# A delta-rule attention and SwiGLU kernel: the loads of v(2), v(3) and K(5) are issued behind the first two pieces of the output weights

## The chip, the cores and the metric

The kernel runs on one core of a Trainium2 chip. The metric is the device time of one execution in microseconds (us), the median of several runs. A profile is one execution taken by the hardware profiler. Its times count from the start of its span.

## What is computed

The reference is a delta-rule recurrence, whose output is reshaped into tokens and sent through a SwiGLU feed-forward block:

```python
# q, k, v: (4, 8, 768, 48) float32; beta: (4, 8, 768) float32
k_n = k / (np.linalg.norm(k, axis=-1, keepdims=True) + 1e-06)
for t in range(S):
    kt, vt, bt = (k_n[:, :, t], v[:, :, t], beta[:, :, t, None])
    y[:, :, t] = np.einsum('bhd,bhde->bhe', q[:, :, t], state)
    v_old = np.einsum('bhde,bhd->bhe', state, kt)
    state = state + bt[:, :, :, None] * np.einsum('bhd,bhe->bhde', kt, vt - v_old)
x = np.ascontiguousarray(y.transpose(0, 2, 1, 3)).reshape(B * S, H * D)
g = x @ w_gate                      # (3072, 384) @ (384, 1536)
silu = g * (1.0 / (1.0 + np.exp(-g)))
out = silu * (x @ w_val) @ w_out    # (1536, 384)
```

The three weight matrices reach the kernel as 64-bit floats, so they are converted to float32 on the chip.

## The kernel before

**Chunks.** The 768 steps are cut into 12 chunks of 64 steps, c = 0 to 11. For each chunk, q, k and v of all 32 heads are loaded, and the recurrence over the chunk is solved with small matrix products. `advance(c)` (line 948 on) is that solution in four steps; its last steps make the 256 tokens of the chunk, which the feed-forward block takes up. "K(5)" below is the load of the k rows of chunk 5, "v(2)" that of the v rows of chunk 2.

**Weights in pieces.** The weights are staged as 42 pieces (`pieces`, lines 200 to 207), numbered in the order of conversion. Pieces 0 to 23 are 128 rows by 256 columns of the gate weights (even numbers) and the value weights (odd numbers). Pieces 24 to 29 are the last 512 columns of both. Pieces 30 to 41 are the twelve 128-row tiles of the output weights. `stage(n)` (line 246) issues the DMA of a piece on SyncE's queue, at line 260, into a place that is shared by several pieces (`place_of`). `freed_by` lists for each piece the pieces that may be staged once it is converted: 24 after 13, 25 after 15, 26 after 17, 28 after 18, 27 after 19, 30 after 21, 31 after 23, 32 after 28, 33 after 29, and from there on each piece after the fourth before it. `freed_by` only places the call; on the chip the DMA itself waits until the last instruction that touches its place is done.

**Conversion.** `convert(ns)` (line 280) converts the pieces of a group. ScalarE does the two activations of `power_step` (lines 272 and 278: the high word scaled into the weight tile, the low word into a "power" tile). VectorE does a shift (line 289), a bit operation (line 297) and the addition of the power (line 309). Between lines 297 and 309, `convert` calls `power_step` for the pieces that follow, so ScalarE takes up a following piece before VectorE's additions for this one. The power tiles are shared: the power of piece 24 lies where those of 22 and 23 lie.

**The first feed-forward chunks.** Chunks 0 and 1 go through `gate_val(c, f, ...)` (line 1402): for two 128-column blocks f and f+1, six matmuls of the gate weights (line 1410), ScalarE's silu (line 1419), six matmuls of the value weights (line 1410), VectorE's product (line 1421). The pairs (c, f) run in the order (0,0), (0,2), (0,4), (0,6), (1,0), (1,2), (1,4), (1,6), (0,8), (1,8), (0,10), (1,10). Their products go round four PSUM banks, two for each pair: the gate product of a pair needs the bank that the silu two pairs earlier has read, the value product the bank that the product at line 1421 two pairs earlier has read. `fill` and `chain` put conversions between the pairs. Then `output` (matmuls at line 1437) multiplies by the output weights for chunks 0 and 1. From chunk 2 on, `gate_val_fast` and `output_fast` do the same with fewer products (matmuls in the helpers at lines 1314 and 1520).

**The inversion.** Each pair of chunks needs a small triangular system inverted (`invert`, line 849). For chunks 2 and 3 it begins between the pairs (0,6) and (1,0): two copies on ScalarE (line 856), two transposes on VectorE (line 569), a power on GpSimd (line 860).

**Order.** Each engine executes its instructions in the order in which the program emits them; the schedule is written by hand. SyncE's queue carries nearly all loads. Each `load_v` is four DMAs (line 186), each `load_k` two (line 140). In `advance(1)`, which is emitted between the conversions of pieces 6 to 17, `load_v(2)` and `load_v(3)` are called at the end of the third step and `load_k(5)` in `of_state` of the fourth.

Of the kernel before, what the change touches and what calls it, by code (L numbers as in the profile page):

```python
# [20 lines left out]
def kernel(  # L21
# [34 lines left out]
    FT = DFF // 128  # L56
# [17 lines left out]
    def ps_pair(name, tag):  # L74

        return pairs_of_banks[tag]
# [19 lines left out]
    AHEAD = 4  # L96
# [12 lines left out]
    def kn_of(c):  # L109
        return knp[c if c < AHEAD else c % 2]  # L110
# [4 lines left out]
    def rows_freed_by(c):  # L115
        return c - AHEAD if c < K_BLOCKS else c - 2
# [18 lines left out]
    def halves(x, c, b):  # L135
        return x[NB * b : NB * b + NB, :, c * C : (c + 1) * C, :]

    def load_heads(t, x, c, dmas=(nc.sync,)):
        for b in range(2):
            dmas[b % len(dmas)].dma_start(  # L140
                out=t[64 * b : 64 * b + 64, :, :, 0:D].rearrange(
                    "p bp h d -> p (bp h) d"
                ),
                in_=halves(x, c, b).rearrange("bp h p d -> p (bp h) d"),
            )

    def load_k(c, dmas=(nc.sync,)):
        load_heads(kn_of(c), k, c, dmas)
# [31 lines left out]
    def load_v(c):  # L180
        vin[c] = work.tile([128, 2, NB, NJ, D], FP32, name="vin", bufs=2)
        for b in range(2):
            src = halves(v, c, b).rearrange("bp (j par) p d -> par p (bp j) d", par=2)
            for par in range(2):
                s = 64 * (b ^ par)
                nc.sync.dma_start(
                    out=vin[c][s : s + 64, par].rearrange("p bp j d -> p (bp j) d"),
                    in_=src[par],
                )
# [10 lines left out]
    pieces = []  # L200
# [6 lines left out]
        pieces.append((wo_sb, moe_w_out, t, 0, DM))  # L207
    assert DFF == 1536 and KT == 3 and DM <= PIECE and 2 * HH * C == 4 * PIECE

    staged, powers, places = {}, {}, {}  # L210

    def words(tile_):
        return tile_.bitcast(U32)

    zt_flat = [words(t).rearrange("p c h i -> p (c h i)") for t in ztp]
    places = {
        "z0": zt_flat[0],
        "z1": zt_flat[1],
        "wo": words(wo_sb).rearrange("p t d -> p (t d)"),
    }  # L220
# [25 lines left out]
    def stage(n, after=None, queue=nc.sync):  # L246
        _, src, t, f0, m = pieces[n]
        name, lo = place_of[n]
        if name not in places:
            if name == "p_sb":  # L250
                places[name] = words(p_places[0])
            else:
                places[name] = work.tile(
                    [128, 2 * PIECE], U32, name="staged", tag=name, bufs=1
                )
        place = places[name][:, lo : lo + 2 * m]
        staged[n] = place
        if after is not None:
            nc.gpsimd.tensor_copy(place[:, 0:1], staged[after][:, 0:1])
        queue.dma_start(  # L260
            out=place, in_=src[t * 128 : (t + 1) * 128, f0 : f0 + m].bitcast(U32)
        )

    def power_step(n):
        if n in powers or n not in staged:
            return
        dst, _, t, f0, m = pieces[n]
        power = words(hp[10 + (n // 2 % 4 if n < N_HALF else (0, 2, 3, 1)[(n + 2) % 4])])
        power = power[:, n % 2 * m : n % 2 * m + m] if n < N_HALF else power[:, 0:m]
        powers[n] = power  # L270
        words_of = staged[n].rearrange("p (f two) -> p f two", two=2)
        nc.scalar.activation(
            dst[:, t, f0 : f0 + m],
            words_of[:, :, 1].bitcast(FP32),
            ACTF.Copy,
            scale=2.0**-112,
        )
        nc.scalar.activation(power, words_of[:, :, 0], ACTF.Copy, scale=2.0**-29)

    def convert(ns, ahead=6):  # L280

        work_of = []
        for n in ns:
            dst, _, t, f0, m = pieces[n]
            power_step(n)
            place = staged.pop(n)[:, 0:m]
            work_of.append((dst[:, t, f0 : f0 + m].bitcast(U32), place, powers.pop(n)))
        for dst, place, _ in work_of:
            nc.vector.tensor_scalar(
                out=place,  # L290
                in0=dst,
                scalar1=3,
                scalar2=None,
                op0=ALU.logical_shift_left,
            )
        for dst, place, _ in work_of:
            nc.vector.scalar_tensor_tensor(
                out=dst,
                in0=dst,
                scalar=0x80000000,  # L300
                in1=place,
                op0=ALU.bitwise_and,
                op1=ALU.bitwise_or,
            )
        for n in range(ns[-1] + 1, ns[-1] + 1 + ahead):
            if n < min(N_HALF, len(pieces)) or ns[-1] + 3 > n < len(pieces):
                power_step(n)
        for dst, _, power in work_of:
            nc.vector.tensor_tensor(out=dst, in0=dst, in1=power, op=ALU.add)  # L309
        for n in ns:  # L310
            for later in freed_by.get(n, ()):
                stage(later)


# [38 lines left out]
    def half_of(x):  # L353
        return slice(64 * x, 64 * x + 64)

    def head_of(x):
        return slice(64 * x, 64 * x + D)

    def every():
        for bp in range(NB):  # L360
            for j in range(NJ):
                for n, (par, b) in enumerate(ORDER):
                    yield bp, j, par, b, bp == 0 and j == 0
# [429 lines left out]
    def recur(p, m=D):  # L793
        p = p[:, :, 0 : NB * NJ * m]
        return p.rearrange("p x (bp j d) -> p x bp j d", bp=NB, j=NJ)
# [152 lines left out]
    def advance(c):  # L948
# [171 lines left out]
                        yield MORE  # L1120
        if c + 2 < NCH:
            if c == 1:
                load_v(2)
                load_v(3)
            elif c > 1:
                late_loads.append(lambda: load_v(c + 2))
        yield
# [15 lines left out]
        def of_state():  # L1143
            p_s = recur(ps_pair("p_s", "px"))
            for bp, j, par, b, first in every():
                nc.tensor.matmul(  # L1146
                    p_s[head_of(par) if c > 0 else half_of(par), b, bp, j],
                    kn[half_of(b), bp, 2 * j + par, 0 : D if c > 0 else DP],
                    uu[half_of(b), par, bp, j],
                    start=first,  # L1150
                    stop=True,
                    skip_group_check=True,
                )
            if c > 0:
                nc.vector.tensor_tensor(out=state, in0=state, in1=p_s, op=ALU.add)
                spent.append(1.4)
            else:
                nc.scalar.copy(state, p_s)
            for later in range(AHEAD, NCH):
                if rows_freed_by(later) == c:  # L1160
                    if c < 2:
                        load_k(later)
                    else:
                        late_loads.append(lambda: load_k(c + 2))

        if 0 < c < NCH - 1:
            of_state()
# [49 lines left out]
        if c == 0:  # L1217
            of_state()
            yield
# [398 lines left out]
    def converts(n):  # L1618
        if todo:
            convert(todo[:n])  # L1620
            del todo[:n]

    def converts_first(*ns):

        convert(list(ns), 0)
        for n in ns:
            todo.remove(n)
# [92 lines left out]
    def point(c):  # L1720

        mine = c < NCH and steps("advance", c) < 4 and may_advance(c)
        if mine and steps("advance", c) > 0:
            step("advance", advance, c)
        elif not prep_step(c - 1) and mine:
            step("advance", advance, c)

    def finish(c):

        if c < NCH:  # L1730
            while not may_advance(c):
                fill_some(1000)
                prep_step(c - 1)
            while steps("advance", c) < 4:
                step("advance", advance, c)
# [196 lines left out]
```

## Time and profile before

| | |
|---|---|
| median of 3 runs | 692.09 us (691.2 to 692.13) |
| the profiled execution | 692.09 us, of which the span of the profile is 690.4 us |
| VectorE busy | 414.0 us (60% of the span) |
| ScalarE busy | 262.6 us (38%) |
| GpSimd busy | 194.3 us (28%) |
| mean rate of the DMAs | 90 GB/s |

The profiled execution took as long as the median, and 1.69 us of it lie outside the span. A row of a timeline has the start and the duration in us, the engine (PE is TensorE, PEld its weight loads, DVE is VectorE, ACT ScalarE, POOL GpSimd, SPq SyncE's queue), the line, the operation, the tile written and the tiles read, shapes, and the number of instructions merged. In brackets stands the idle time of the engine just before, and what ended it. A tile is named by its memory: `zt`, `wo_sb`, `p_sb` and `staged` are the places into which weight pieces are loaded, `h_f` and `last_h` those of powers and hidden values, `vin` v, `kn` k.

### The profile page before, as it was taken

To read this page: it belongs to the slowest core of one execution; us is meant where nothing else is said; L and a number is where in the kernel's file an instruction comes from. 1 tells how busy PE (TensorE), PEld (TensorE's weight loads), DVE (VectorE), ACT (ScalarE), POOL (GpSimd) and SP (SyncE) were. 2 spreads that over 40 slices of the span, in tenths; PEclk is the share of its full clock that TensorE was granted. 3 is DMA by queue.
4 is the path that set the end of the run, shared out by engine and by line. 5 is a ranking of instruction groups with operands and counts; after the bars stand their busy time and mean duration, and the time that the engine had idled before them with its cause. 6 is when DMAs were issued, how large, how long until landed. Compare 5 with 4: busy or idle time off the path is not lost.

```text
span 690.4 us, 24601 instructions
## 1 busy us (share of the span) xinstructions
PE 675.4 (98%) x10836; PEld 629.7 (91%) x10836; DVE 414.0 (60%) x874; ACT 262.6 (38%) x557; POOL 194.3 (28%) x310
## 2 busy tenths in 40 slices
PE   8899999999999999999999999999999999999997
PEld 4788788756999999999999999999999999999997
DVE  7888578898657664647456546655555544433341
ACT  4777576214432523344323245232144242142230
POOL 5111031105883128820037830308810000000000
PEclk9999999999999999999999999999999999999999
DMA  9658925017561621464432373253253121221210
GB/s 133 160 162 204 245 75 161 1 34 174 129 113 19 116 79 40 100 110 93 88 77 71 69 137 73 56 103 77 55 110 69 56 64 47 56 63 47 71 45 24
DMA packets 143851, 62.24 MB, mean 90 GB/s; under 512 B 122977, under 2 KB 126049, under 8 KB 143745
## 3 DMA queue, kind: packets, MB, share of 16 engines
q1 hardware_dynamic: 141536, 60.19, 38.5%
q8 instruction: 85, 1.39, 0.9%
q10 hardware_dynamic: 2080, 0.39, 0.4%
q0 software_dynamic: 128, 0.10, 0.1%
q14 instruction: 22, 0.17, 0.1%
HBM read 53.58 MB, written 7.08 MB: 88 GB/s over the span
## 4 chain that ended last, share of the span: by engine, by line
PE 82%; DMA 8%; ACT 3%; SPq 3%; DVE 2%; issue 1%; POOL 0%; POOLq 0%; DVEq 0%; ACTq 0%
PE ffn L1314 42%; PE ffn L1520 20%; PE ffn L1437 4%; DMA h_f<-in_moe_w_val_dram 2%; PE ffn L1410 2%; PE p_px L977 2%; PE p_py L960 2%; DMA wo_sb<-in_moe_w_val_dram 2%; SPq L140 1%; PE p_py L1134 1%; PE p_px L1043 1%; PE p_px L1146 1%; PE p_px L527 1%; PE p_py L1207 1%; DMA wo_sb<-in_moe_w_gate_dram 1%
## 5 line engine op out<-in xcount | busy, mean ns | idle before, releaser
L1314 PE MATMUL ffn<-x_ffn,wg_sb 128*128 128x128 f32 x840 | 128.4, 275 | 0.5 <-ACT ffn L1370 0.3
L1314 PE MATMUL ffn<-x_ffn,wv_sb 128*128 128x128 f32 x840 | 128.1, 275 | 0.0
L1314 PEld LDWEIGHTS ffn<-x_ffn,wg_sb 128*128 128x128 f32 x840 | 111.1, 192 | 1.0 <-ACT ffn L1370 0.7
L1314 PEld LDWEIGHTS ffn<-x_ffn,wv_sb 128*128 128x128 f32 x840 | 110.7, 192 | 0.0
L1349 DVE TENSOR_TENSOR h_f<-sil,ffn 128x256 f32<-128x256 f32 x120 | 49.6, 418 | 83.6 <-ACT sil L1344 82.2
L1344 ACT ACTIVATE sil<-ffn 128x256 f32<-128x256 f32 x120 | 45.8, 383 | 128.1 <-PE ffn L1314 127.3
L1520 PE MATMUL ffn<-wo_sb,h_f 128*128 128x192 f32 x480 | 83.4, 327 | 0.0
L860 POOL TENSOR_TENSOR n_b<-mb,half 128x32 f32<-128x32 f32 x5 | 30.0, 6005 | 178.2 <-DVE mb L569 178.2
L1520 PEld LDWEIGHTS ffn<-wo_sb,h_f 128*128 128x128 f32 x480 | 78.1, 190 | 0.3
L605 POOL TENSOR_TENSOR zb<-zb,tmp 128x31 f32<-128x31 f32 (+15 forms) x124 | 72.6, 586 | 9.7
L599 POOL TENSOR_TENSOR tmp<-zb,mb 128x31 f32<-128x31 f32 (+15 forms) x124 | 67.0, 540 | 16.9 <-DVE mb L586 7.4
L1481 DVE TENSOR_TENSOR ffn<-ffn,p_sb 128x512 f32<-128x512 f32 x58 | 40.4, 696 | 48.7 <-ACT ffn L1370 47.3
L1314 PE MATMUL ffn<-x_t,h_f 128*128 128x128 f32 x480 | 61.0, 280 | 0.2 <-ACT ffn L1327 0.2
L1314 PEld LDWEIGHTS ffn<-x_t,h_f 128*128 128x128 f32 x480 | 56.3, 191 | 2.1 <-ACT ffn L1327 0.4
L1481 DVE TENSOR_TENSOR o_sb<-o_sb,ffn 128x192 f32<-128x192 f32 x49 | 17.2, 352 | 64.0 <-PE ffn L1520 61.4
L1327 ACT COPY ffn<-ffn 128x512 f32<-128x512 f32 x30 | 17.1, 571 | 60.8 <-PE ffn L1314 60.8
L1410 PE MATMUL ffn<-x_ffn,wg_sb 128*128 128x256 f32 x144 | 34.5, 385 | 2.9 <-DVE wg_sb L309 1.4
L1478 DVE TENSOR_TENSOR h_f<-h_f,h_f 128x256 f32<-128x256 f32 x60 | 29.6, 496 | 11.8 <-PE ffn L1520 10.6
L1520 PE MATMUL ffn<-last_k,h_f 128*128 128x192 f32 x200 | 36.0, 327 | 0.0
L1410 PE MATMUL ffn<-x_ffn,wv_sb 128*128 128x256 f32 x144 | 33.9, 383 | 0.4 <-DVE h_f L1421 0.4
L1410 PEld LDWEIGHTS ffn<-x_ffn,wg_sb 128*128 128x128 f32 x144 | 26.5, 190 | 7.6 <-DVE wg_sb L309 2.2
L1520 PEld LDWEIGHTS ffn<-last_k,h_f 128*128 128x128 f32 x200 | 32.9, 190 | 0.1
(323 smaller groups left out, 1123.3 us busy)
## 6 DMA issues: line engine op xcount, KB each, us to landing
h_f<-w_s SPq DMA_DIRECT2D x60, 256.0 KB, 2.8
p_sb<-w_s SPq DMA_DIRECT2D x27, 256.0 KB, 2.8
vin<-in_v_dram SPq DMA_DIRECT2D x48, 96.0 KB, 3.3
out_dram<-o_sb SPq DMA_DIRECT2D x48, 96.0 KB, 2.2
kn<-in_k_dram SPq DMA_DIRECT2D x20, 192.0 KB, 4.8
zt<-in_moe_w_out_dram SPq DMA_DIRECT2D x6, 384.0 KB, 3.8
qpad<-in_q_dram SPq DMA_DIRECT2D x36, 64.0 KB, 3.1
w_s<-h_f SPq DMA_DIRECT2D x7, 256.0 KB, 4.2
```

The lines of the kernel that those rows point to most:

```text
L599: engine.tensor_tensor(out=t_v, in0=zb[:, 0 : j + 1, j : j + 1].to_broadcast([128, j + 1, m]), in1=mb[:, j : j + 1, j + 1 : R].to_broadcas ...
L605: engine.tensor_tensor(out=zb[:, 0 : j + 1, j + 1 : R], in0=zb[:, 0 : j + 1, j + 1 : R], in1=t_v, op=ALU.add,)
L860: nc.gpsimd.tensor_tensor(out=n, in0=mb.rearrange("p j i -> p (j i)")[:, 0 : R * R : R + 1], in1=half, op=ALU.pow,)
L1314: nc.tensor.matmul(p[:, u], w(u), moving, start=start and u == 0, stop=True, skip_group_check=True,)
L1327: nc.scalar.copy(p_y, p_x)
L1344: nc.scalar.activation(sil[:, n].rearrange("p (i n) -> p i n", i=2), p[:, 0:2], ACTF.Silu)
L1349: nc.vector.tensor_tensor(out=h_of(c, f, j), in0=sil[:, n].rearrange("p (i n) -> p i n", i=2), in1=p[:, 2:4], op=ALU.mult,)
L1410: nc.tensor.matmul(ps[name][:, i], w_sb[:, t, (f + i) * 128 : (f + i + 1) * 128], xts[c][:, t], start=(t == 0 and i == 0), stop=(t == KT - 1),
L1437: nc.tensor.matmul(p_o, hs[c, f - f % 2][:, f % 2, bp * 128 : (bp + 1) * 128], wo_sb[:, f], start=(f == 0), stop=(f == FT - 1),)
L1478: nc.vector.tensor_tensor(out=out, in0=a, in1=b, op=ALU.subtract)
L1481: nc.vector.tensor_tensor(out=out, in0=a, in1=b, op=ALU.add)
L1520: nc.tensor.matmul(p[x, part], a(f - f % 2)[:, f % 2], b(f), start=not begun and f == 0, stop=f == FH - 1, skip_group_check=True,)
```

## The change

The three loads are no longer issued where `advance(1)` reaches them. They are put into a list, `held`, and issued from `convert`, just before piece 32 (the third piece of the output weights) is staged: `len(pieces) - FT + 2` is 42 - 12 + 2 = 32. The list is emptied from its end, so K(5) comes first, then v(2), then v(3). All other instructions and their order stay.

```diff
-    staged, powers, places = {}, {}, {}
+    staged, powers, places, held = {}, {}, {}, []
...
         for n in ns:
             for later in freed_by.get(n, ()):
+                if later == len(pieces) - FT + 2:
+                    while held:
+                        held.pop()()
                 stage(later)
...
         if c + 2 < NCH:
             if c == 1:
-                load_v(2)
-                load_v(3)
+                held.append(lambda: (load_v(2), load_v(3)))
             elif c > 1:
                 late_loads.append(lambda: load_v(c + 2))
...
             for later in range(AHEAD, NCH):
                 if rows_freed_by(later) == c:
-                    if c < 2:
+                    if c == 0:
                         load_k(later)
+                    elif c == 1:
+                        held.append(lambda: load_k(AHEAD + 1))
                     else:
                         late_loads.append(lambda: load_k(c + 2))
```

## The prediction

> **What bounds the kernel now.** First the page's first part, then the busy time of the engines in four stretches (columns: stretch, its length, busy time and instructions of each engine, granted clock, DMA share, GB/s).
>
> ```profile
> span 690.4 us, 24601 instructions
> PE 675.4 (98%) x10836; PEld 629.7 (91%) x10836; DVE 414.0 (60%) x874; ACT 262.6 (38%) x557; POOL 194.3 (28%) x310
> ...
> 64.00:129.00 65.00, 61.84 (x552) 53.12 (x549) 49.77 (x113) 40.26 (x76) 10.39 (x6) 1.00 0.51 146
> 129.00:175.00 46.00, 44.96 (x705) 29.50 (x704) 40.27 (x96) 11.59 (x21) 12.38 (x10) 1.00 0.35 84
> 175.00:690.00 515.00, 510.95 (x7864) 501.52 (x7862) 273.20 (x530) 168.33 (x359) 156.17 (x251) 1.00 0.35 75
> ```
>
> TensorE sets the time. It is idle for 3.16 us between 64 and 129 us, where the weights are converted, for 1.04 us of the next 46 us and for 4.05 us of the last 515 us, at a granted clock of 1.00. All instructions ahead of the first moved load stay where they are, so an edit of load order can gain little more than those 3.16 us. The timeline of TensorE shows what they are.
>
> ```profile
> 76.45 1.13 PE L1410 MATMUL ffn<-x_ffn,wg_sb 128*128 128x256 f32 x4
> 79.02 1.99 PE L1410 MATMUL ffn<-x_ffn,wg_sb 128*128 128x256 f32 x8 [1.43 <-DVE wg_sb L309]
> ...
> 96.96 2.86 PE L1410 MATMUL ffn<-x_ffn,wv_sb 128*128 128x256 f32 x12 [0.41 <-DVE h_f L1421]
> ...
> 104.84 2.75 PE L1410 MATMUL ffn<-x_ffn,wg_sb 128*128 128x256 f32 x12
> ...
> 111.36 2.86 PE L1410 MATMUL ffn<-x_ffn,wg_sb 128*128 128x256 f32 x12 [1.18 <-ACT sil L1419]
> ...
> 116.65 1.04 PE L511 MATMUL p_px<-ident,kn 128*128 128x128 f32 x8
> ```
>
> Three waits: 1.43 us inside the gate product of pair (0,6), 0.41 us before the value product of (1,4), 1.18 us before the gate product of (1,8): 3.02 us. The first waits for VectorE's addition for piece 22. Next, the timeline of VectorE, then that of ScalarE.
>
> ```profile
> 64.71 0.42 DVE L297 SCALAR_TENSOR_TENSOR wv_sb<-wv_sb,wo_sb 128x256 uint32<-128x256 uint32 x1
> ...
> 74.61 0.69 DVE L1421 TENSOR_TENSOR h_f<-sil,ffn 128x512 f32<-128x512 f32 x1 [3.83 <-PE ffn L1410]
> ...
> 76.49 0.42 DVE L297 SCALAR_TENSOR_TENSOR wv_sb<-wv_sb,zt 128x256 uint32<-128x256 uint32 x1
> 76.82 0.42 DVE L309 CUSTOM_DVE_ANT_0 wv_sb<-wv_sb,last_h 128x512 uint16<-128x512 uint16 x1
> 78.54 0.42 DVE L309 CUSTOM_DVE_ANT_0 wg_sb<-wg_sb,last_h 128x512 uint16<-128x512 uint16 x1 [1.29 <-ACT last_h L278]
> 78.88 0.42 DVE L309 CUSTOM_DVE_ANT_0 wv_sb<-wv_sb,last_h 128x512 uint16<-128x512 uint16 x1
> ...
> 92.34 2.25 DVE L569 STREAM_TRANSPOSE mb<-a_sb 128x512 f32<-128x512 f32 x2 [4.19 <-ACT a_sb L856]
> ...
> 96.23 0.68 DVE L1421 TENSOR_TENSOR h_f<-sil,ffn 128x512 f32<-128x512 f32 x1
> ...
> 160.21 0.96 DVE L474 TENSOR_TENSOR vin<-vin,n_t 128x768 f32<-128x768 f32 x1
> ```
>
> ```profile
> 71.95 0.60 ACT L1419 ACTIVATE sil<-ffn 128x512 f32<-128x512 f32 x1 [1.41 <-PE ffn L1410]
> 77.30 0.66 ACT L272 ACTIVATE wg_sb<-wo_sb 128x512 f32<-128x512 f32 x1 [4.75 <-DMA wo_sb<-in_moe_w_gate_dram]
> ...
> 80.66 0.67 ACT L272 ACTIVATE wv_sb<-wo_sb 128x512 f32<-128x512 f32 x1 [2.15 <-DMA wo_sb<-in_moe_w_val_dram]
> ...
> 84.52 0.60 ACT L1419 ACTIVATE sil<-ffn 128x512 f32<-128x512 f32 x1
> ...
> 88.41 3.89 ACT L856 COPY a_sb<-a_sb 32x1024 f32<-32x1024 f32 x2
> 92.33 0.60 ACT L1419 ACTIVATE sil<-ffn 128x512 f32<-128x512 f32 x1
> ...
> 101.64 0.56 ACT L272 ACTIVATE wo_sb<-staged 128x384 f32<-128x384 f32 x1 [4.03 <-DMA staged<-in_moe_w_out_dram]
> ...
> 103.45 0.57 ACT L1419 ACTIVATE sil<-ffn 128x512 f32<-128x512 f32 x1
> ```
>
> So the addition for piece 22 stands still for 1.29 us until ScalarE has written a power tile: that of piece 24, which shares its memory and comes first in the program. ScalarE in turn sat idle for 4.75 us until piece 24 had landed, and 2.15 us more for piece 25. Both were late because of SyncE's queue:
>
> ```profile
> 63.88 0.44 SPq L260 DMA_DIRECT2D p_sb<-in_moe_w_val_dram  x1
> 64.37 7.33 SPq L186 DMA_DIRECT2D vin<-in_v_dram  x8
> 71.81 0.56 SPq L260 DMA_DIRECT2D wo_sb<-in_moe_w_gate_dram  x1
> 72.47 1.32 SPq L140 DMA_DIRECT2D kn<-in_k_dram  x2
> 73.89 3.00 SPq L260 DMA_DIRECT2D wo_sb<-in_moe_w_val_dram  x1
> 77.00 1.86 SPq L260 DMA_DIRECT2D wo_sb<-in_moe_w_gate_dram  x1
> 78.91 0.42 SPq L260 DMA_DIRECT2D staged<-in_moe_w_gate_dram  x1
> 79.44 0.37 SPq L260 DMA_DIRECT2D wo_sb<-in_moe_w_val_dram  x1
> 79.91 1.66 SPq L260 DMA_DIRECT2D zt<-in_moe_w_out_dram  x2
> 98.25 0.33 SPq L260 DMA_DIRECT2D staged<-in_moe_w_out_dram  x1
> ...
> SPq L260 <- DVE wg_sb L297: 16.6, 1, 16.6
> ...
> DMA to landing us min/median/max: 3.2/5.0/7.6
> ```
>
> In order these are piece 29, v(2) and v(3), piece 24, K(5), pieces 25, 26, 28, 27, then 30 and 31, and piece 32 after a wait of 16.6 us for the conversion of piece 28. The last row gives the landing times of line 260's DMAs between 54 and 120 us.
>
> **The change, part by part.** *Removed from ahead of 24 and 25:* ten DMAs, 7.33 + 1.32 = 8.65 us of issue. Piece 24 can issue at about 64.4 (it waits only for the conversion of 13, ahead of that of 15). Even with the longest landing above it is there at 64.4 + 7.6 = 72.0; ScalarE wants it at 71.95 + 0.60 = 72.55. Piece 25 waits for line 297 of piece 15, 64.71 + 0.42 = 65.13, and is there by 72.8 at the latest; ScalarE wants it one pair of activations later. Three such pairs and the silu fill 84.52 to 88.41, so a pair is (3.89 - 0.57)/3 = 1.1 us, and 25 is wanted at 73.7. Both ScalarE idles go.
>
> *First wait of TensorE.* VectorE's additions then follow one another at 0.34 us, as 78.54 and 78.88 do. The second starts at 76.82 + 0.34 = 77.16 and ends at 77.58. TensorE has finished its four matmuls at 76.45 + 1.13 = 77.58, so about 0.05 us of hand-over remains: gain 1.43 - 0.05 = 1.38. Bounds: 0 if the row's releaser is wrong, 1.43 if nothing remains.
>
> *Second.* The value product of (1,4) waits for line 1421 of (1,0) at 96.23, which stands behind the transposes at 92.34, which wait for line 856 on ScalarE. From 80.66 to 96 ScalarE runs almost without a gap, so its lateness there is the lateness of pieces 24 and 25. Without it, the silu of (0,6) comes when its gate product is ready: 79.02 + 1.99 - 1.38 = 79.63, against 84.52. ScalarE is free by then: the four copies between piece 25's pair, 80.66 + 1.1 = 81.8, and 84.5 need 2.7 us and can start once the small products ahead of 76.45 are done. So line 856 and the transposes come 84.52 - 79.63 = 4.9 us earlier, and line 1421 of (1,0) ends near 96.23 + 0.68 - 4.9 = 92.0. TensorE wants the bank at 96.96 - 0.41 - 1.38 = 95.2. It is there 3.2 us before: gain 0.41.
>
> *Third.* The silu that is missed at 111.36 is that of (1,6), which stands on ScalarE behind the power of piece 36. That piece was staged after the conversion of 32, itself staged after that of 28. All of these hang on the chain just described. Piece 32 took 101.64 - 98.25 = 3.39 us from issue to use; with the issue 4.9 us earlier, near 93.4, the silu of (1,6) is done 4.9 us earlier and the bank is free at 111.36 - 4.9 = 106.5. TensorE wants it at 111.36 - 1.18 - 1.38 - 0.41 = 108.4. Gain 1.18, with 1.9 us to spare.
>
> *Added behind piece 31:* the ten DMAs. Piece 31 waits for line 297 of piece 23, which ends at 76.91, and SyncE, now without a backlog, issues it at about 77.3. The ten then take the 8.65 us that they took before: done by 86.0, at the latest 86.0 + 7.6 = 93.6 landed. They lie in the 16.6 us in which SyncE stood waiting, so they cost nothing. Without that cover, what they delay is piece 32 (below). Their users are far off: K(5) at 116.65, v(2) at 160.21. Their buffers are free by then: before, the queue issued v from 64.37 and K(5) at 72.47.
>
> *Sum:* 1.38 + 0.41 + 1.18 = 2.97 us. After 129 us TensorE is idle 1.04 us in 46 and 4.05 in 515, so the work behind follows it; that stretch could return some of the gain only if another engine's chain became late, and VectorE and ScalarE move forward by more than TensorE does. The profiled execution has 692.09 us, its span 690.4, and is itself the median: 692.09 - 2.97 = 689.1. The bounds of the terms are 0 and 3.16 us, and about 0.5 us more if some of the idle time behind goes too.
>
> **The rivals.** *(1) Only the first two waits go:* the third returns because the chain 28, 32, 36 doesn't come forward by the 2.97 us that it needs (the forecast has 4.9). Against it: each link in the rows is a wait for the one before. Time: 692.09 - 1.79 = 690.3.
>
> *(2) Hidden anyway:* the early pieces find the DMA engines so full that they land no sooner, or the gain is lost in a later stage that something other than TensorE times. For it: a DMA share of 0.51 on average here, with landings of up to 7.6 us. Against it: 7.6 us is enough, and TensorE is 98% busy after. Time: 692.1.
>
> *(3) Slower: piece 32 is late.* Place: SyncE's queue between 31 and 32. If the ten loads don't slip into the 16.6 us but wait as 32 does, or their small rows still occupy the rings when 32 is issued, 32 goes out at 93.4 + 8.65 = 102.0. The silu of (1,4) came 103.45 - 101.64 = 1.81 us after the use of 32 began, so TensorE's gate product of (0,8) would start near 102.0 + 3.39 + 1.81 + 0.6 = 107.8 instead of 104.84 - 1.79 = 103.05. The cost of 4.8 us turns -1.79 into +3.0: 695.1. It decides once 32 is issued after 97.2 (103.05 - 5.8), and the total is above before's from about 99. Against it: SyncE reaches 32 by 86. The Trainium skill speaks for this rival (page "DMA: Bandwidth & Descriptors", section "Queues, rings and completion order"): SyncE owns one row of rings, and on each DMA engine descriptors are consumed in ring order, so piece 32 cannot pass the ten loads. By that rule alone it costs what is left of them at 93.4, by the latest landing above 0.2 us, which the 1.9 us to spare take up; no run here shows it yet.
>
> *(4) It doesn't do what it says:* if piece 32 were released before `advance(1)` is emitted, the loads would go nowhere near. The rows exclude it: K(5) is issued ahead of 25, 32 well behind.
>
> **How the numbers follow.** Forecast 0.74 (688.6 to 689.7), rival 1 0.12, rival 2 0.08, rival 3 0.05, rival 4 0.01. The predicted time is the forecast's, 689.1. The range runs from 688.4 (all bounds favourable) to 691.2, which takes in rival 1 with its second gain lost too, 692.09 - 1.38 = 690.7, and the 0.5 us by which the runs of before lie apart around their median. What can be told from no change here is about 0.2%, 1.4 us: forecast and nearly all of rival 1 are faster (0.85), rival 2 and the rest of rival 1 the same (0.10), rival 3 slower (0.05).
>
> **What would show it.** Right: SyncE's queue has 24 and 25 directly behind 29, and kn and vin behind the two zt rows, with a wait before 32 that is still several us long; ScalarE's idle of 4.75 us before line 272 is gone, the silu of (0,6) stands near 79.7, line 856 near 83.6; TensorE has no wait above 0.1 us between 64 and 126, where the output products (line 1437) now start, 3 us sooner than the stretch boundary of 129 above. Wrong: a new wait of ScalarE for pieces 24 to 28 (rival 2), a wait left before the gate product of (1,8) (rival 1), piece 32 issued after 97 (rival 3), or a TensorE that starts line 1437 3 us earlier and ends at the same time, which would say that a later stage is timed by something else.

## The result, and the profile after

| | before | after |
|---|---|---|
| median | 691.33 us (689.94 to 692.13, 8 runs) | 687.48 us (687.05 to 690.3, 8 runs) |
| the profiled execution | 692.09 us, span 690.4 us | 690.3 us, span 688.6 us |
| ratio, 95% interval | | 0.9951 (0.9936 to 0.9966) |

The ratio is a gain of 3.4 us (2.4 to 4.4). The forecast was 689.1 us, and its range, 688.4 to 691.2, does not hold the measured 687.48.

The two profiled executions differ by less than the medians, 1.8 us. To see why, compare the busy time in stretches (columns as in the prediction). This is the profile after:

```profile
0.00:64.00 64.00, 57.66 (x1595) 45.57 (x1596) 48.56 (x130) 42.34 (x101) 15.02 (x44) 0.95 0.79 167
64.00:126.00 62.00, 61.82 (x671) 53.68 (x670) 51.81 (x119) 40.65 (x76) 10.41 (x6) 1.00 0.50 146
...
175.00:688.00 513.00, 509.16 (x7848) 499.71 (x7846) 272.61 (x529) 168.08 (x358) 154.74 (x247) 1.00 0.34 75
```

Between 64 and 126 us TensorE is now idle for 0.18 us. In the first 64 us, where both programs are the same, this execution had a granted clock of 0.95. TensorE's timeline:

```profile
78.55 3.17 PE L1414 MATMUL ffn<-x_ffn,wg_sb 128*128 128x256 f32 x12
81.55 2.75 PE L1414 MATMUL ffn<-x_ffn,wv_sb 128*128 128x256 f32 x12
...
107.45 2.75 PE L1414 MATMUL ffn<-x_ffn,wv_sb 128*128 128x256 f32 x12
110.04 2.75 PE L1414 MATMUL ffn<-x_ffn,wg_sb 128*128 128x256 f32 x12
...
127.75 2.42 PE L1441 MATMUL ffn<-wo_sb,h_f 128*128 128x384 f32 x7
```

(After the change the lines stand 3 or 4 further down: 1410 is 1414, 1437 is 1441, 1419 is 1423.) No wait is left. The gate product of (0,6) starts 2.10 us later than before (78.55 against 76.45), the first output product 1.42 us sooner (127.75 against 129.17). I call the time between these two starts **the stretch**: 49.20 us against 52.72 us, a gain of 3.52 us. SyncE's queue and ScalarE after the change:

```profile
60.81 1.81 SPq L260 DMA_DIRECT2D p_sb<-in_moe_w_val_dram  x1
64.80 0.33 SPq L260 DMA_DIRECT2D wo_sb<-in_moe_w_gate_dram  x1
67.41 0.33 SPq L260 DMA_DIRECT2D wo_sb<-in_moe_w_val_dram  x1
...
78.39 1.00 SPq L260 DMA_DIRECT2D zt<-in_moe_w_out_dram  x2
79.48 1.31 SPq L140 DMA_DIRECT2D kn<-in_k_dram  x2
80.85 7.63 SPq L186 DMA_DIRECT2D vin<-in_v_dram  x8
95.53 0.34 SPq L260 DMA_DIRECT2D staged<-in_moe_w_out_dram  x1
```

```profile
74.04 0.60 ACT L1423 ACTIVATE sil<-ffn 128x512 f32<-128x512 f32 x1 [1.41 <-PE ffn L1414]
74.53 0.65 ACT L272 ACTIVATE wg_sb<-wo_sb 128x512 f32<-128x512 f32 x1
...
75.64 0.67 ACT L272 ACTIVATE wv_sb<-wo_sb 128x512 f32<-128x512 f32 x1
...
81.75 0.60 ACT L1423 ACTIVATE sil<-ffn 128x512 f32<-128x512 f32 x1 [1.28 <-PE ffn L1414]
...
85.66 3.93 ACT L859 COPY a_sb<-a_sb 32x1024 f32<-32x1024 f32 x2
...
106.64 0.58 ACT L1423 ACTIVATE sil<-ffn 128x512 f32<-128x512 f32 x1
```

Pieces 24 and 25 go out at 64.8 and 67.4, ScalarE takes them up without a wait, and ahead of the silu of (0,6) it now waits for TensorE instead of for a DMA. The last row is the silu of (1,6): it ends at 107.22, 2.8 us before the gate product of (1,8) starts at 110.04. The ten loads lie between 79.5 and 88.5, and SyncE still has 7 us before piece 32 at 95.53.

### The profile page after: what moved, and what is told of

It is laid out like the page before. It is cut to its first block, busy times and chain, and to the rows that moved or that the text cites. A ratio compares the mean times of both kernels' runs of the same rounds, so it can differ in the third digit from the quotient of the medians.

```text
span 688.6 us, 24605 instructions
## 1 busy us (share of the span) xinstructions
PE 677.0 (98%) x10836; PEld 631.7 (92%) x10836; DVE 414.0 (60%) x874; ACT 263.2 (38%) x557; POOL 194.0 (28%) x310
## 4 chain that ended last, share of the span: by engine, by line
PE 89%; DMA 3%; SPq 3%; ACT 2%; DVE 1%; issue 1%; POOL 0%; DVEq 0%; POOLq 0%; ACTq 0%
PE ffn L1318 43%; PE ffn L1524 20%; PE ffn L1414 8%; PE ffn L1441 4%; PE p_px L980 2%; DMA h_f<-in_moe_w_val_dram 2%; PE p_py L963 2%; PE p_py L1136 1%; PE p_px L1046 1%; PE p_px L1148 1%; SPq L140 1%; PE p_px L530 1%; PE p_py L1211 1%; SPq L186 1%; PE p_px L924 1%
```

## The experiments

Each row is one profile, of one execution. "Start" is the start of the gate product of (0,6), "stretch" the time from there to the first output product, "rest" the time from there to the end of the span, all from the timelines of TensorE. "Clock" is the granted clock between 32 and 40 us. The ratio is that of a kernel's times to times of the kernel before that were taken beside them.

| kernel | start | stretch | rest | clock | ratio, 95% interval |
|---|---|---|---|---|---|
| before | 76.45 | 52.72 | 561.23 | 0.79 | |
| before, 2nd profile | 75.57 | 52.91 | 561.52 | 1.00 | |
| before, 3rd profile | 75.43 | 51.88 | 562.29 | 1.00 | |
| after | 78.55 | 49.20 | 560.85 | 0.57 | 0.9951 (0.9936 to 0.9966) |
| after, 2nd profile | 74.86 | 49.20 | 561.34 | 1.00 | 0.9936 (0.9917 to 0.9956) |
| v alone held | 78.05 | 49.20 | 561.05 | 0.79 | 0.9960 (0.9945 to 0.9975) |
| K alone held | 74.64 | 50.15 | 561.11 | 1.00 | 0.9973 (0.9960 to 0.9986) |
| own powers | 74.44 | 51.12 | 560.94 | 1.00 | 0.9991 (0.9977 to 1.0004) |
| held until 26 | 74.28 | 50.72 | 560.60 | 1.00 | 0.9980 (0.9966 to 0.9994) |
| held until 33 | 75.24 | 56.00 | 561.06 | 1.00 | 1.0040 (1.0024 to 1.0057) |
| GpSimd's queue | 79.18 | 49.20 | 561.82 | 1.00 | 1.0015 (1.0000 to 1.0030) |
| gate piece first | 75.60 | 48.89 | 561.61 | 1.00 | 0.9945 (0.9926 to 0.9965) |

**The two kernels again.** The changed kernel:

> The changed kernel again, for a second profile. Theory (the profiled execution of the changed kernel was 2.1 us late before 64 us, where nothing differs): the stretch from the small products at 76.5 of that profile to the first output product takes 51.2 us again, against 54.7 us before, and the start of the small products moves by up to 2 us between profiles. Rival (moving the loads also slows the first 64 us): they start at 76.5 again, within 0.3 us.

The stretch takes 49.20 us again, to the hundredth, and starts at 74.86 instead of 78.55. So the theory holds, though the start moved by 3.7 us where up to 2 were expected: nothing here shows that moving the loads slows the first 64 us. The kernel before, twice:

> The kernel before again, for a second profile. Theory (the stretch from the gate product of (0,6) to the first output product is set by the late pieces, the same in each execution): 52.7 us again, within 0.2 us, while the start of that stretch moves with the granted clock of the first 64 us. Rival (the third wait of the first profile came from one long landing of piece 36, 5.3 us from issue to use against 3.5 in other profiles): 51.1 to 52.2 us, with the third wait smaller or gone.

> As the run before it, a third profile of the kernel before: 52.7 us by the theory, 51.1 to 52.2 us by the rival.

The waits of TensorE in the second profile of before, then in the third:

```profile
77.53 1.99 PE L1410 MATMUL ffn<-x_ffn,wg_sb 128*128 128x256 f32 x8 [0.83 <-DVE wg_sb L309]
...
92.66 2.86 PE L1410 MATMUL ffn<-x_ffn,wg_sb 128*128 128x256 f32 x12 [0.18 <-ACT sil L1419]
96.65 2.86 PE L1410 MATMUL ffn<-x_ffn,wv_sb 128*128 128x256 f32 x12 [1.14 <-DVE h_f L1421]
...
110.67 2.86 PE L1410 MATMUL ffn<-x_ffn,wg_sb 128*128 128x256 f32 x12 [0.80 <-ACT sil L1419]
```

```profile
78.37 1.99 PE L1410 MATMUL ffn<-x_ffn,wg_sb 128*128 128x256 f32 x8 [1.81 <-DVE wg_sb L309]
...
96.55 2.86 PE L1410 MATMUL ffn<-x_ffn,wv_sb 128*128 128x256 f32 x12 [0.65 <-DVE h_f L1421]
```

Here the theory that the stretch is the same each time falls: 52.72, 52.91 and 51.88 us, a mean of 52.50. The first two waits trade with one another: where the first is short (0.83), the second is long (1.14). They are one lateness, taken up at two places. The third wait follows the rival's mechanism: from its issue to its use, piece 36 took 5.28 us in the first profile (104.57 to 109.85), 4.88 in the second and 3.62 in the third, and the wait is 1.18, 0.80 and none. So it needs both the late chain and a long landing. The changed kernel doesn't owe its absence to a short landing: piece 36 took 3.87 us there, and 1.4 us more would still leave the silu of (1,6) 1.4 us ahead of its need. Against 49.20 the gain is 3.30 us on average, 2.7 to 3.7 by execution, which agrees with the 3.4 us of the ratio. The rival's time fits the third profile only.

**Which of the loads.** In the changed kernel, only v(2) and v(3) held:

```diff
-                    if c == 0:
-                        load_k(later)
-                    elif c == 1:
-                        held.append(lambda: load_k(AHEAD + 1))
+                    if c < 2:
+                        load_k(later)
```

> Only v(2) and v(3) are held back; K(5) stays where it was. Theory (one chain: ScalarE gets pieces 24 and 25 late, because SyncE has 8.65 us of issue ahead of them): 7.33 of the 8.65 us go, piece 25 is issued 1.3 us later than in the changed kernel and still lands before ScalarE wants it, so nearly all of the gain is there: 3.2 to 3.5 us less than the kernel before, and no TensorE wait between 64 and 126. Rival (the transfers of all three loads count alike, K(5) with a third of the bytes): about 2.3 us less.

Or only K(5):

```diff
-                held.append(lambda: (load_v(2), load_v(3)))
+                load_v(2)
+                load_v(3)
```

> Only K(5) is held back; v(2) and v(3) stay where they were. Theory (one chain): piece 24 still lands near 77.2, so the first TensorE wait stays, but ScalarE's second wait of 2.15 us, for piece 25, goes, and the chain behind it comes about 2 us sooner: the second wait goes and the third shrinks or goes, 1.5 to 1.9 us less than the kernel before. Rival (a share by issue time, 1.32 of 8.65): 0.5 us less.

With v alone held, the stretch is 49.20: the whole gain, as the theory expected (by the times 2.8 us, 1.7 to 3.8). With K alone held, one wait is left, the first:

```profile
76.77 1.99 PE L1415 MATMUL ffn<-x_ffn,wg_sb 128*128 128x256 f32 x8 [0.99 <-DVE wg_sb L309]
```

Its stretch is 50.15, 2.35 us below before's mean; by the times 1.9 us (1.0 to 2.8). So two DMAs of 1.3 us of issue bring more than half of what eight DMAs of 7.3 us bring, and the two gains add up to far more than the whole. ScalarE takes up piece 25 1.68 us after the start of the stretch (76.32), against 4.21 before, and the silu of (0,6) follows at 5.54 (80.18), against 8.07: 2.5 us sooner each, so once 25 is on time, much of the chain is. A share by issue time (0.5 us) is excluded.

**The power tile that 22, 23 and 24 share.** In the kernel before, with the loads in their old place:

```diff
-        power = words(hp[10 + (n // 2 % 4 if n < N_HALF else (0, 2, 3, 1)[(n + 2) % 4])])
+        power = words(hp[10 + (n // 2 % 4 if n < N_HALF else (3, 2, 1, 0)[(n + 2) % 4])])
```

By the order of the program, the additions for 22 and 23 then read their own powers; before, and in the changed kernel too, they read what the power of 24 had left in that memory. The instructions are the same.

> The loads stay as before; the power tiles of the pieces from 24 on are dealt out in another order, so that the power of 24 no longer lies where those of 22 and 23 lie, and VectorE's addition for piece 22 no longer waits for piece 24. Theory (one chain): the first TensorE wait goes (1.4 us of idle), but ScalarE still waits for 24 and 25 as long, so the second wait grows from 0.4 to about 2 us: no change in time, within 0.4 us. Rival (three waits that each cost their own): 1.4 to 1.8 us less.

The waits of TensorE in the stretch:

```profile
90.81 2.86 PE L1410 MATMUL ffn<-x_ffn,wg_sb 128*128 128x256 f32 x12 [0.25 <-ACT sil L1419]
94.80 2.86 PE L1410 MATMUL ffn<-x_ffn,wv_sb 128*128 128x256 f32 x12 [1.13 <-DVE h_f L1421]
```

The first wait is gone and two others are there, of 0.25 and 1.13 us. The silu of (1,0), behind line 856, comes 15.72 us after the start of the stretch, against 15.88 (92.33 - 76.45), 16.43 and 16.46 in the three profiles of before, so the chain is nearly as late as it was. The third wait is gone, but so it is in the third profile of before, where the powers are the old ones: piece 36 took 3.50 us from issue to use here. The stretch is 51.12, 1.4 us below before's mean; the times say 0.6 us less, between 1.6 less and 0.3 more. Over half of this 1.4 is the third wait, whose share of the stretch, counted by start-to-start distances as in the section on the prediction, was 1.45, 1.07 and 0 us in the three profiles of before. Without it, the three stretches of before are 2.1, 2.6 and 2.7 us longer than the changed kernel's, and this one 1.9. So, as far as one profile shows, removing the first wait (1.40, 0.79 and 1.77 us of those) was worth some 0.5 us on average, and the rest of it was taken up at the second place. That lies nearer to the theory than to the rival.

**Only 24 and 25 ahead.**

```diff
-                if later == len(pieces) - FT + 2:
+                if later == len(pieces) - FT - 4:
```

> All three loads are held, but only until just before piece 26: 24 and 25 go ahead of them, 26, 28, 27, 30 and 31 behind. Theory (24 and 25 are what is late): piece 26 is issued some 6 us later than in the changed kernel and lands up to 2 us after ScalarE first wants it, which the 1.9 us to spare mostly takes up: 2.5 to 3.5 us less than the kernel before. Rival (all weight pieces count): a new wait of ScalarE for 26 to 28 of 4 us or more, and less than 1 us gained.

SyncE's queue, ScalarE and TensorE in this run:

```profile
64.37 1.77 SPq L140 DMA_DIRECT2D kn<-in_k_dram  x2
66.19 9.25 SPq L186 DMA_DIRECT2D vin<-in_v_dram  x8
75.55 0.56 SPq L260 DMA_DIRECT2D wo_sb<-in_moe_w_gate_dram  x1
```

```profile
79.89 0.68 ACT L272 ACTIVATE wg_sb<-wo_sb 128x512 f32<-128x512 f32 x1 [1.80 <-DMA wo_sb<-in_moe_w_gate_dram]
...
83.44 0.67 ACT L272 ACTIVATE wv_sb<-wo_sb 128x512 f32<-128x512 f32 x1 [2.32 <-DMA wo_sb<-in_moe_w_val_dram]
```

```profile
94.24 2.86 PE L1414 MATMUL ffn<-x_ffn,wv_sb 128*128 128x256 f32 x12 [1.13 <-DVE h_f L1425]
```

Less was gained than expected: a stretch of 50.72, by the times 1.4 us (0.4 to 2.3). The ten loads took 11 us here, not 8.7, and ScalarE waits 1.80 us for piece 26 and 2.32 us more for 27, together 4.12 us, the rival's "4 us or more" and over twice the 1.9 us that I had to spare. The second wait of TensorE is back at 1.13 us. The gain lies between the two expectations: it is not 24 and 25 alone, 26 and 27 count too.

**Behind piece 32: the slower rival made real.**

```diff
-                if later == len(pieces) - FT + 2:
+                if later == len(pieces) - FT + 3:
```

> The loads are held one piece longer, until just before piece 33, so they stand on SyncE's queue behind the wait of piece 32. This is the slower rival's mechanism made real. By its price: piece 33 is issued 8.7 us later than in the changed kernel, the silu of (1,4) comes near 109 instead of 100.6, TensorE waits about 4.8 us before the gate product of (0,8); 5 us more than the changed kernel, 1.0 to 1.8 us more than the kernel before. Rival (ScalarE has enough done ahead): no more than 1 us over the changed kernel.

TensorE's timeline, ScalarE's, and the busy time in stretches of 2 us, with the granted clock third from the end:

```profile
105.98 5.13 PE L1414 MATMUL ffn<-x_ffn,wg_sb 128*128 128x256 f32 x12 [4.26 <-ACT sil L1423]
110.94 2.75 PE L1414 MATMUL ffn<-x_ffn,wv_sb 128*128 128x256 f32 x12
```

```profile
104.46 0.54 ACT L272 ACTIVATE wo_sb<-p_sb 128x384 f32<-128x384 f32 x1 [7.91 <-DMA p_sb<-in_moe_w_out_dram]
```

```profile
102.00:104.00 2.00, 0.00 (x0) 0.00 (x0) 0.00 (x0) 0.00 (x0) 0.00 (x0) 0.95 0.95 323
104.00:106.00 2.00, 0.02 (x1) 0.02 (x1) 0.53 (x2) 1.54 (x4) 0.00 (x0) 0.50 0.63 250
...
108.00:110.00 2.00, 2.00 (x7) 1.55 (x6) 1.93 (x5) 0.48 (x2) 0.00 (x0) 0.50 0.85 320
```

The place is the one that the rival named, and the wait, 4.26 us, is close to the 4.8 expected. The cost is larger: the stretch is 6.8 us longer than the changed kernel's, and the time 2.8 us (1.7 to 3.9) above the kernel before, not 1.0 to 1.8. The rest goes with the clock: it fell to 0.50 during the wait, and the twelve matmuls behind took 5.13 us instead of 2.75.

**The loads on GpSimd's queue, at their old place.**

```diff
-                load_v(2)
-                load_v(3)
+                load_v(2, nc.gpsimd)
+                load_v(3, nc.gpsimd)
...
-                    if c < 2:
+                    if c == 0:
                         load_k(later)
+                    elif c == 1:
+                        load_k(later, (nc.gpsimd,))
```

(The lines that give `load_v` its queue as an argument are left out here.)

> The three loads stay at their old place in the program, but are issued from GpSimd's queue instead of SyncE's. Theory (issue time on SyncE's queue is what is late): pieces 24 and 25 are issued at once, and 3 to 3.5 us go. Rival (the transfers themselves crowd the DMA engines, whoever issues them): 24 and 25 are issued early but land after 72.5 and 73.7, and less than 1.8 us goes.

The DMA issues between 55 and 90 us (count, size of one, median us to landing), then ScalarE's timeline and TensorE's:

```profile
wo_sb<-in_moe_w_gate_dram SPq DMA_DIRECT2D x2, 512.0 KB, 12.3
wo_sb<-in_moe_w_val_dram SPq DMA_DIRECT2D x2, 512.0 KB, 13.5
vin<-in_v_dram POOLq DMA_DIRECT2D x8, 96.0 KB, 6.9
```

```profile
71.04 0.43 ACT L272 ACTIVATE wv_sb<-zt 128x256 f32<-128x256 f32 x1 [5.21 <-DMA zt<-in_moe_w_val_dram]
```

```profile
67.70 0.70 PE L658 MATMUL p_px<-half 32*32 32x1 f32 x64 [2.84 <-issue]
...
70.75 3.88 PE L1412 MATMUL ffn<-x_ffn,wg_sb 128*128 128x256 f32 x12
```

GpSimd issues the loads from 57.09 us on. With SyncE's queue free, the weight pieces go out as early as in the changed kernel (24 at 62.77, as in the second profile of that kernel), but take 12 to 13.5 us to land, where there the medians are 5.5 and 5.7. ScalarE takes up piece 24 at 75.66, there at 70.84, though TensorE is level with that profile until 63.8 us (line 1209 starts at 63.75, line 1211 there at 63.78). So the piece is used 4.8 us later, about as late as in the kernel before, where ScalarE waited 4.75 us for it. The stretch of 49.20 doesn't show this, because it begins at 79.18, 4.3 us later than in that profile: TensorE waited 2.84 us at line 658, where there it waited 0.24, and then had a clock of 0.50 from 70 to 72, so its gate product took 3.88 us instead of 2.75. The profile names no releaser for that wait, so whether the loads caused it stays open; ScalarE's 5.21 us for piece 23 ended later, and no wait of TensorE follows from it. The time is the kernel before's or slightly more (1.0015). So the theory that issue time alone matters is wrong, and the rival is right that the pieces land late: the loads must also not be in the DMA engines ahead of the weights. In the changed kernel their place behind piece 31 settles both at once. The Trainium skill says (page "DMA: Bandwidth & Descriptors", section "Issuing engines are not separate DMA queues") that DMAs of all engines interleave on the same 16 DMA engines, and that issuing from several saves only issue time. The landings of 12.3 and 13.5 us agree.

**What is left at the first wait.** On top of the change, the addition for piece 22 goes first in its group:

```diff
+        if ns == [21, 22, 23]:
+            work_of = [work_of[i] for i in (1, 0, 2)]
         for dst, _, power in work_of:
```

> The changed kernel, and in the group of pieces 21, 22, 23 VectorE's addition for the gate piece 22 comes first. Theory (start-to-start spacing counts, not the idle in brackets): in the changed kernel the gate product of (0,6) still takes 3.00 us to the next product instead of 2.59, though no idle is shown; with the addition 0.34 us sooner it takes 2.65 to 2.7. 0.3 us less than the changed kernel, too little to tell by the times. Rival: spacing stays 3.00.

TensorE's timeline:

```profile
75.60 2.86 PE L1416 MATMUL ffn<-x_ffn,wg_sb 128*128 128x256 f32 x12
78.29 2.75 PE L1416 MATMUL ffn<-x_ffn,wv_sb 128*128 128x256 f32 x12
```

The two starts lie 2.69 us apart instead of 3.00, and the stretch is 48.89 us, 0.31 us less, as expected. It is the shortest of all; by the times (0.9945) it can't be told from the changed kernel.

## Why the prediction was right about the cause and wrong about the number

**Right.** The queue of SyncE, ScalarE's missing wait for 24 and 25, the silu of (0,6), line 856 and the three waits of TensorE all came out as described. Counted from the start of the gate product of (0,6), the silu was forecast at 79.63 - 76.45 = 3.18 us and came at 3.20; line 856 was forecast at 7.1 and came at 7.11. The ten loads cost nothing in the 16.6 us of SyncE's wait. Whether piece 32 could have passed loads still under way, which the third rival denies, no run shows: it went out at 95.53, 7 us after the last of them. Nothing of the gain was given back: the rest after the stretch is 560.6 to 562.3 us in all twelve profiles. Of the rivals, the partial gain, the hidden gain and the slower one didn't happen; the slower one's place was shown real by the run that held the loads until piece 33.

**Wrong: the size of the terms.** The step that failed is "1.38 + 0.41 + 1.18 = 2.97 us", which took the idle time in brackets for the cost of a wait. The start-to-start distance of equal groups shows more. These rows of the kernel before stand beside those of the prediction:

```profile
80.85 2.75 PE L1410 MATMUL ffn<-x_ffn,wv_sb 128*128 128x256 f32 x12
...
93.80 2.75 PE L1410 MATMUL ffn<-x_ffn,wg_sb 128*128 128x256 f32 x12
...
99.66 2.75 PE L1410 MATMUL ffn<-x_ffn,wg_sb 128*128 128x256 f32 x12
...
107.43 2.75 PE L1410 MATMUL ffn<-x_ffn,wv_sb 128*128 128x256 f32 x12
...
114.06 2.75 PE L1410 MATMUL ffn<-x_ffn,wv_sb 128*128 128x256 f32 x12
...
129.17 22.09 PE L1437 MATMUL ffn<-wo_sb,h_f 128*128 128x384 f32 x68
```

An undisturbed group of twelve takes 2.59 us (107.45 to 110.04 after). In the profile before, the gate product of (0,6) took 80.85 - 76.45 = 4.40 us to the next, 1.81 more; it still took 3.00 after, so 1.40 were gained. That this is so close to the forecast 1.38 is luck: the wait cost 1.81 us, not 1.43, and 0.41 of it stayed, not 0.05. The group before the second wait took 96.96 - 93.80 = 3.16, 0.57 more; the group before the third 111.36 - 107.43 = 3.93, 1.34 more; and the two groups behind these waits took 2.70, 0.11 more each. That makes 1.40 + 0.57 + 1.34 + 0.22 = 3.53 for the stretch's 3.52. So the second and the third wait each took 0.27 us more than their idle. Both parts of that stand in the rows: a group lasts 2.75 us but the next one starts 2.59 after it, an overlap of 0.16 that is lost at a wait, and the group behind a wait lasts 2.86, 0.11 more. The waits of the weight loads in the profile before hint at a reason, which wasn't tried by itself:

```profile
PEld ffn L1410 <- DVE wg_sb L309: 1.8, 1, 1.8
PEld ffn L1410 <- ACT sil L1419: 1.6, 1, 1.6
...
PEld ffn L1410 <- DVE h_f L1421: 0.8, 1, 0.8
```

The weight loads, which otherwise run ahead of the matmuls (after, at 81.34 for the group of 81.55), stood for 4.2 us where the matmuls show 3.02.

**Wrong: one execution taken for the kernel.** The sum started from 692.09, the profiled execution, which was also the median of three runs. Over eight runs the median is 691.33. Of the 1.62 us by which the forecast missed, 0.76 are this base and 0.55 the size of the terms, which leaves 687.8; the other 0.3 lie within the spread of the runs. The three waits were one draw too: the mean stretch of three profiles is 52.50, not 52.72, and with its gain of 3.30 us the sum is 688.0. The range put 0.5 us of spread on its upper side only and let the lower end rest on the "3.16 us" of idle and 0.5 us of idle behind. The distances above show that idle is no bound: the stretch gained 3.52.

**Half right: three waits as three terms.** In the sum they add up. But the first two are one lateness: where one is short, the other is long, and with its own powers the kernel kept most of it at the second place. The third hangs on the same chain and on how long piece 36 takes to land, which the prediction left out: its 1.18 us are gone in one of three profiles of the kernel before.

## What to carry to other kernels

A wait's cost is read from the start-to-start distance of equal groups against an undisturbed one, not from the idle in brackets. When several waits hang on one late chain, ask what is late at its head, for removing a wait in its middle moves most of it on. On a shared queue the order of loads decides twice, by issue time and by how long the loads ahead keep the next ones from landing: what is needed late goes where the queue stands waiting anyway. Before a range is written, take the spread of the whole runs on both sides; one profile is one draw.

## What the runs showed of the hardware

Over the twelve profiles, the stretch starts between 74.28 and 79.18 us, while what follows it takes 560.6 to 562.3. The granted clock between 32 and 40 us was 0.57, 0.79 or 1.00, and the start moved with it: 78.55 at 0.57 and 74.86 at 1.00 for the same program. (At 79.18 it was 1.00, and the delay came later.) In the first of these two, the 64 and the 128 matmuls of line 1075 (1072 before) begun at 32.22 and 35.64 us took 3.65 and 5.39 us; in the second, those begun at 31.67 and 33.54 took 2.07 and 3.93. By starts, that is 3.0 of the 3.7 us between the two.

A short idle time was enough for the clock to fall. In the run that was held until piece 33, the last matmul before the wait ended at 101.72, the clock fell to 0.50 near 103.8, 2.1 us later, and it was back at 1.00 by 111, some 4.6 us after work began again. The Trainium skill has a rule for this (page "TensorE: Matmul & The Clock Gate", section "Part 1: The HAM clock gate"): after an idle window of about 3.4 us TensorE's clock is halved until it has been busy for such a window, and the windows run freely, so the same kernel can hit or miss one. The halving agrees with these runs, but a full 3.4 us of idle was not needed; how the windows lay in time, no run here shows. Ahead of 32 us, too, no wait is that long: 1.06 and 0.81 us in the execution that lost the clock, 0.39 and 0.81 in the one that kept it. Why the first 64 us sometimes lose the clock was not tried.
